# Gated mix of cached attention and a small gated MLP, one decode step: W_down's load ahead of the third K tile, the first K tile loaded from two queues

## The chip, the cores and the metric

The kernel runs on one core of one Trainium2 chip. The core has TensorE (PE), VectorE (DVE), ScalarE (ACT), GpSimd (POOL) and SyncE (SP), and 16 transfer engines (DMA) that move data between HBM and the on-chip memory. Here SyncE and ScalarE issue transfers, each in its own queue. The metric is the device time in microseconds; lower is better. A profile has its own, single execution, whose time need not be the median of the timed runs.

## The reference

One token (x, 448 values) goes through an attention block with a cache of 65,536 positions, 8 key/value heads and 16 query heads of size 256, and through a small gated MLP. A scalar gate mixes both results.

```python
x = A_x
g = sigmoid((x * gate_w).sum(-1, keepdims=True))
# attention: Hq = 16, Hkv = 8, Sk = 65536, Dh = 256
q = (x @ wq).reshape(1, 1, 16, 256)
p = softmax(q . k_cache * 256 ** -0.5)     # each K head serves two query heads
a = (p @ v_cache).reshape(1, 1, 4096) @ wo
# MLP: F = 1792
b = (relu(x @ W_gate) * (x @ W_up)) @ W_down
return g * a + (1 - g) * b
```

K and V are 256 MB each in binary megabytes (8 x 65,536 x 256 values of 2 bytes). The weights are small beside them: wq and wo 3.5 MB each, the three MLP matrices about 1.5 MB each.

## The kernel before

**Tiles and buffers.** K and V of every head are cut into four tiles (NTH = 4), 32 K tiles and 32 V tiles in all (NT = 32). A tile is 128 partitions by 64 KB, 8 MB. Three buffers of that size, `ring[0]` to `ring[2]`, hold what is loaded. K tiles alternate between `ring[1]` and `ring[2]` (`place`, L406): K0 in `ring[1]`, K1 in `ring[2]`, K2 in `ring[1]` again, and so on. V tiles, but for the last four, go to `ring[0]`. Before the first V tile, `ring[0]` holds the weights side by side: wq in its front part (L346, L347), W_gate and W_up in that same part once the query is made (L350, L351), and W_down behind wq (L349), in a part that nothing else uses until the MLP is over.

**The order of the loads.** The list `order` (L381) names the loads in the order in which SyncE issues them, each with its planned duration in us. From it follow the due times `tL`. SyncE's program is in that order, and an issue that has to wait holds up every issue behind it. K tile n (L680) waits until the scores of tile n - 2 are made, since it overwrites that buffer (`free`, L564). W_gate and W_up (L640, L642) wait until the query is made. W_down (L675) waits for nothing. V0 (L772) waits until the MLP is over.

**The order on the engines.** Every operation has an engine and a key; each engine's program is sorted by key (`finish`), and waits on semaphores are put in where an operation depends on another engine or on a transfer. So an engine works strictly in the order of the keys. ScalarE's queue begins with the loads of x (L421, key -9) and of gate_w (L422, key -8), 0.9 KB each.

**What happens to the first K tile.** VectorE begins with constants (keys below 0.1), then makes x's transposed copies with TensorE (L478 to L494, keys 0.5 to 0.91, from x), then the gate: product with gate_w (L464, key 1), sum, exponential on ScalarE (L466), reciprocal and difference (L468 to L470), a broadcast through TensorE (L471, L472) and L475 (key 1.9). Behind these come the four transposes of K0 in place (L682 with `f_trans`, keys from 22.35 on). TensorE meanwhile multiplies x by wq (`f_q`, L497 to L503), ScalarE copies the query (L630), VectorE turns it (L632) and spreads it (`f_xm`), ScalarE copies it to `xcur` (L634), and TensorE makes the scores (`f_qk`, L531 to L544) in two halves. VectorE takes the maximum of each row (L703) and ScalarE the exponential (L705). Then follow the transposes of K1.

Every fourth K tile closes a head: the maxima are brought together, the probabilities scaled and transposed, and the products with V (L584) follow as the V tiles land. At the end come the last V tile in three pieces, wo in six, and the output.

Of the kernel before, what the change touches and what calls it, by code (L numbers as in the profile page):

```python
# [27 lines left out]
class _Plan:  # L28
# [8 lines left out]
    def op(self, eng, key, fn, deps=(), tag=None):  # L37
        eng, cls = {"pv": ("pe", "pv"), "dx": ("dv", "dx"), "ap": ("ac", "ap")}.get(eng, (eng, eng))
        o = _Op(eng, key, fn, deps, tag=tag, cls=cls)
        self.ops.append(o)  # L40
        return o

    def dma(self, eng, key, sem, fn, deps=()):
        if sem not in self.dsem:
            self.dsem[sem] = self.es.enter_context(self.nc.semaphore("d_" + sem))
        o = _Op(eng, key, fn, deps, dma=sem)
        self.ops.append(o)
        return o
# [212 lines left out]
def bass_gated_mix__gqa_block_cached__glu_gated_reglu__decode_kernel(  # L261
# [35 lines left out]
    with es:  # L297
# [3 lines left out]
        ring = [sb("ring%d" % i, [128, U * DH], BF) for i in range(NRING)]  # L301
# [69 lines left out]
        op, dma = pl.op, pl.dma  # L371
# [6 lines left out]


        TILE = 19.35  # L380
        order = [("k", 0, TILE), ("wq", 0, 8.7), ("k", 1, TILE), ("k", 2, TILE), ("wd", 0, 3.8), ("gu", 0, 7.7)]  # L381
        for n in range(3, NT):
            order.append(("k", n, TILE))
            if n >= NTH:
# [10 lines left out]
        t = 3.0  # L395
# [10 lines left out]
        def place(kind, i):  # L406
            if kind == "k":
                return 1 + i % 2
            if kind == "v":
                return 1 + i % 2 if i >= NT - NTH else 0  # L410
            return {"vp": 2, "wo": 0}[kind]

        for kind, i, _ in order:
            if kind in ("k", "v") or (kind, i) in (("wo", 0), ("vp", 0)):
                r = place(kind, i)
# [101 lines left out]
        def k_src(n):  # L517
            h, t_ = divmod(n, NTH)
            return A_k_cache[0, h, :, :].rearrange("(p t u) d -> p t (u d)", t=NTH, u=U)[:, t_, :]
# [7 lines left out]
        def f_trans(sl, w):  # L527
            v = ring[sl][:, w * 8192:(w + 1) * 8192].bitcast(U32)
            return lambda e: e.transpose(v, v)  # L529
# [34 lines left out]
        def free(key):  # L564
            out_ = []
            for f in freed[key]:
                out_.append(l_[f] if isinstance(f, str) else qk[f[1], 1] if f[0] == "k" else pv[f[1]])
            return out_
# [55 lines left out]
        for kind, i, t in sorted(issue, key=lambda q: q[0] != "wq"):  # L624
# [51 lines left out]
            elif kind == "k":  # L676
                n = i
                h, t_ = divmod(n, NTH)
                sl = slot["k", n]
                kd = dma("sp", t, "r%d" % sl, lambda e, n=n, sl=sl: e.dma_start(ring[sl][:], k_src(n)), free(("k", n)))  # L680
                tk = max(tL["k", n], last.get("free", 0))
                tr = [op("dv", tk + 4.5 * w, f_trans(sl, w), [kd]) for w in range(4)]  # L682
                if n > 1:
                    tr[1].deps.append(aexp[n - 2])
                if t_ == 0:
# [82 lines left out]
            elif kind in ("v", "vp"):  # L768
                if kind == "v":
                    n, lo, hi = i, 0, U  # L770
                    sl = slot["v", n]
                    dep = dma("sp", t, "r%d" % sl, lambda e, sl=sl, n=n: e.dma_start(ring[sl][:], v_src(n)), free(("v", n)))  # L772
                else:
                    n, (lo, hi) = NT - 1, PIECES[i]
                    sl = slot["vp", 0]
# [96 lines left out]
```

## Time and profile before

| | |
|---|---|
| time, median of 3 runs | 1278.07 us (1277.55 to 1278.48) |
| time of the profiled execution | 1279.05 us |
| its span | 1277.2 us |
| HBM read in the span | 549.03 MB, 430 GB/s |
| VectorE busy | 630.0 us (49%) |
| TensorE busy | 359.1 us (28%) |
| ScalarE busy | 78.0 us (6%) |

The span goes from the first to the last instruction of the core; the profiled execution's time is 1.85 us longer. The strips of the page show the span in 40 slices of about 32 us, with a digit for each tenth of busy share. In the lists, a row begins with its start and its duration in us, then come the engine and the line of the kernel, and what ended the idle time before it. A "q" behind an engine's name (SPq, ACTq) marks what that engine's sequencer issues, here transfers. The views of stretches give busy time per engine, then the granted clock of TensorE, the share of the 16 transfer engines, and the rate.

### The profile page before, as it was taken

Reading aid. Unit: us, or ns where it says so; the run is one execution under the profiler, and the core shown is the slowest. Engines: PE = TensorE matmul, PEld = TensorE weight load, DVE = VectorE, ACT = ScalarE, POOL = GpSimd, SP = SyncE. Lnnn points to the kernel's source line nnn. Section 1 sums busy time; section 2 is a strip of 40 time slices with the busy share of each in tenths; the row PEclk is TensorE's granted clock in tenths of the full one; section 3 lists DMA queues with packets and bytes.
Section 4 is the critical chain, followed back from the end, with each engine's and each line's share of the span. In section 5 each row is a group of like instructions: output and inputs, shape, how many; then the busy total and the mean of one; then the engine's idle time right before and its main releaser. Section 6 shows DMA issues by size and latency. Waiting matters only on the chain.

```text
span 1277.2 us, 10244 instructions
## 1 busy us (share of the span) xinstructions
PE 359.1 (28%) x4505; PEld 150.8 (12%) x4505; DVE 630.0 (49%) x309; ACT 78.0 (6%) x163; POOL 4.6 (0%) x23
## 2 busy tenths in 40 slices
PE   0533420142220323212322321233302233202525
PEld 0111110021100111101111110111100111001202
DVE  4776655553555633557334575335554355554300
ACT  0000100010000100001000010000000010000100
POOL 1000000000000000000000000000000000000000
PEclk9756655666655666656666556666556666566667
DMA  9999999999999999999999999999999999999998
GB/s 411 395 438 433 429 427 433 443 435 429 427 433 441 437 429 427 433 441 435 431 427 433 441 435 431 427 433 443 433 431 427 435 441 433 431 427 435 441 418 364
DMA packets 11389, 549.13 MB, mean 430 GB/s; under 512 B 1267, under 2 KB 1654, under 8 KB 2294
## 3 DMA queue, kind: packets, MB, share of 16 engines
q1 hardware_dynamic: 11378, 549.03, 99.5%
q8 instruction: 4, 0.07, 0.0%
q14 instruction: 3, 0.02, 0.0%
q10 hardware_dynamic: 4, 0.00, 0.0%
HBM read 549.03 MB, written 0.00 MB: 430 GB/s over the span
## 4 chain that ended last, share of the span: by engine, by line
DMA 80%; PE 15%; DVE 3%; ACT 1%; issue 1%; SPq 0%; another core or an unknown queue 0%; ACTq 0%
DMA ring<-in_A_v_cache_dram 74%; PE O L584 13%; DMA ring<-in_A_wo_dram 3%; DVE ring L529 3%; DMA ring<-in_A_wq_dram 2%; PE ST L540 1%; ACT pcur L591 1%; PE O L501 1%; SPq L785 0%; PE A_ps L551 0%; SPq L776 0%; DVE nmb L703 0%; DVE ring L660 0%; PE A_ps L653 0%
## 5 line engine op out<-in xcount | busy, mean ns | idle before, releaser
L529 DVE STREAM_TRANSPOSE ring<-ring 128x4096 uint32<-128x4096 uint32 x128 | 557.5, 4413 | 207.5 <-DMA ring<-in_A_k_cache_dram 207.5
L584 PE MATMUL O<-ring,pcur 128*4 128x512 bf16 x2048 | 179.5, 527 | 795.8 <-ACT pcur L591 786.9
L703 DVE TENSOR_REDUCE nmb<-ST 128x1 f32<-128x512 f32 x32 | 22.1, 692 | 339.2 <-PE ST L540 339.2
L584 PEld LDWEIGHTS O<-ring,pcur 128*4 128x4 bf16 x2048 | 57.6, 108 | 917.9 <-ACT pcur L591 803.2
L540 PE MATMUL ST<-ring,xcur 128*16 128x512 bf16 x2048 | 136.5, 419 | 47.9 <-DVE ring L529 47.3
L540 PEld LDWEIGHTS ST<-ring,xcur 128*16 128x16 bf16 x2048 | 64.5, 92 | 113.6 <-DVE ring L529 51.8
L705 ACT ACTIVATE P_sb<-ST,nmb 128x512 bf16<-128x512 f32 x32 | 44.5, 1392 | 362.7 <-DVE nmb L703 362.7
L591 ACT COPY pcur<-ptp 128x256 bf16<-128x256 bf16 x32 | 13.2, 415 | 741.1 <-DMA ring<-in_A_v_cache_dram 741.1
L607 DVE TENSOR_SCALAR o_sb<-O,rcm 128x256 bf16<-128x256 f32 x8 | 3.8, 478 | 60.9 <-PE O L584 60.9
L730 DVE TENSOR_TENSOR P_sb<-P_sb,hs 128x1024 bf16<-128x1024 bf16 x16 | 18.9, 1222 | 7.9 <-ACT hs L724 7.9
L735 PE MATMUL PT<-identb,P_sb 128*128 128x128 bf16 x128 | 14.3, 279 | 17.5 <-DVE P_sb L730 17.3
L501 PE MATMUL O<-ring,P_sb 128*128 128x512 bf16 x28 | 8.6, 479 | 17.6 <-DMA ring<-in_A_wq_dram 17.6
L735 PEld LDWEIGHTS PT<-identb,P_sb 128*128 128x128 bf16 x128 | 10.4, 124 | 19.9 <-DVE P_sb L730 19.9
L744 ACT COPY ptp<-PT 128x256 bf16<-128x256 bf16 x32 | 10.3, 375 | 22.7 <-PE PT L735 22.7
L705 ACT ACTIVATION_READ_ACCUMULATOR P_sb<-ST,nmb 128x1 f32 x32 | 8.3, 258 | 0.0
L501 PEld LDWEIGHTS O<-ring,P_sb 128*128 128x128 bf16 x28 | 3.2, 118 | 22.5 <-issue 20.7
L551 PE MATMUL A_ps<-ring,attnA 128*1 128x224 bf16 x64 | 5.2, 319 | 1.2 <-DMA ring<-in_A_wo_dram 1.1
L756 DVE RECIPROCAL rc<-M_ps 128x2 f32<-128x2 f32 x8 | 1.4, 170 | 7.5 <-PE M_ps L755 7.5
L719 PE MATMUL M_ps<-identf,hs 128*2 128x128 f32 x8 | 2.2, 270 | 9.9 <-DVE hs L717 9.9
L571 PE MATMUL O<-zer,identb 128*128 128x512 bf16 x8 | 4.7, 587 | 0.0
L755 PE MATMUL M_ps<-hs,ones_f 128*128 128x2 f32 x16 | 4.5, 352 | 0.0
L557 PE MATMUL A_ps<-o_sb,ecur 128*128 128x32 bf16 x64 | 3.2, 191 | 3.1 <-DVE o_sb L610 3.1
(94 smaller groups left out, 69.9 us busy)
## 6 DMA issues: line engine op xcount, KB each, us to landing
ring<-in_A_v_cache_dram SPq DMA_DIRECT2D x1, 4096.0 KB, 23.6
ring<-in_A_wq_dram SPq DMA_DIRECT2D x1, 3072.0 KB, 29.0
ring<-in_A_v_cache_dram SPq DMA_DIRECT2D x1, 3072.0 KB, 30.6
ring<-in_B_W_down_dram SPq DMA_DIRECT2D x1, 1568.0 KB, 25.8
ring<-in_B_W_gate_dram SPq DMA_DIRECT2D x1, 1344.0 KB, 28.1
ring<-in_B_W_up_dram SPq DMA_DIRECT2D x1, 1344.0 KB, 30.1
ring<-in_A_wo_dram SPq DMA_DIRECT2D x1, 1232.0 KB, 34.7
ring<-in_A_v_cache_dram SPq DMA_DIRECT2D x1, 1024.0 KB, 32.2
```

The costliest lines, as they stand in the source:

```text
L501: ins = e.matmul(QN_ps, xw3[:, kt, 31 - m:159 - m], rhs, start=(kt == 0 and m == 0), stop=(kt == R3 and m == J // 4 - 1))
L529: return lambda e: e.transpose(v, v)
L540: ins = e.matmul(bank[32 * w:32 * w + 16, :], xcur[:, x0:x0 + 16], ktv[sl][:, u0:u0 + 16, c, :, r_], start=(b == 0 and c == 0 and r_ == 0) ...
L551: ins = e.matmul(A_ps[32 * g:32 * g + 1, 0:D2], lhsT, rhs[:, g * D2:(g + 1) * D2], start=start, stop=stop, skip_group_check=True, tile_pos ...
L571: last["zo", h] = op("pv", key, lambda e: e.matmul(OP[:], identb[:, :], zer[:, 0:1].to_broadcast([128, 512]), start=True, stop=True, skip_ ...
L584: ins = e.matmul(OP[32 * g:32 * g + 4, :], pcur[a % 2][:, 4 * k:4 * k + 4], ring[sl][:, k * 512:(k + 1) * 512], start=False, stop=False, s ...
L591: pc[n] = op("ap", max(tp - 5, last["tev", h] - 0.5), lambda e: e.copy(pcur[a % 2][:].rearrange("p (k i) -> p k i", i=4), ptp[:].rearrange ...
L703: smax[n] = op("dv", sx, lambda e, n=n, t_=t_: e.tensor_reduce(NM[:, t_:t_ + 1], ST[n % 2][:], AX.X, ALU.max, negate=True), [qk[n, 1], las ...
L705: aexp[n] = op("ac", sx + 1, lambda e, n=n, t_=t_: e.activation(P_sb[:, t_:2048:4], ST[n % 2][:], ACTF.Exp, bias=NM[:, t_:t_ + 1], scale=1 ...
L730: rsc = op("dv", tt, lambda e, pb=pb: e.tensor_tensor(pb, pb, X[:, 12:16].unsqueeze(1).to_broadcast([128, 256, 4]), ALU.mult), [h7, aexp[n]])
L735: ins = e.transpose(PT[rd][:, s * 128:(s + 1) * 128], P_sb[:, (rd * 8 + s) * 128:(rd * 8 + s + 1) * 128], identb[:, :])
L744: ins = e.copy(dst, src)
```

## The change

Two edits. In `order`, W_down (`wd`) changes places with K2, so that SyncE issues it behind K1 and ahead of K2. And K0 is no longer issued as one transfer of 128 partitions: SyncE issues partitions 0 to 63 in its old place, and ScalarE issues partitions 64 to 127, with key -10 and a semaphore of its own (`k0`). The transposes of K0 depend on both transfers. The other K tiles are issued as before.

```diff
-        order = [("k", 0, TILE), ("wq", 0, 8.7), ("k", 1, TILE), ("k", 2, TILE), ("wd", 0, 3.8), ("gu", 0, 7.7)]
+        order = [("k", 0, TILE), ("wq", 0, 8.7), ("k", 1, TILE), ("wd", 0, 3.8), ("k", 2, TILE), ("gu", 0, 7.7)]
...
-                kd = dma("sp", t, "r%d" % sl, lambda e, n=n, sl=sl: e.dma_start(ring[sl][:], k_src(n)), free(("k", n)))
+                rows_ = slice(0, 64 if n == 0 else 128)
+                kd = dma("sp", t, "r%d" % sl, lambda e, n=n, sl=sl, rows_=rows_: e.dma_start(
+                    ring[sl][rows_, :], k_src(n)[rows_, :]), free(("k", n)))
+                kds = [kd] if n else [kd, dma("ac", -10, "k0", lambda e, sl=sl: e.dma_start(ring[sl][64:128, :], k_src(0)[64:128, :]))]
                 tk = max(tL["k", n], last.get("free", 0))
-                tr = [op("dv", tk + 4.5 * w, f_trans(sl, w), [kd]) for w in range(4)]
+                tr = [op("dv", tk + 4.5 * w, f_trans(sl, w), kds) for w in range(4)]
```

## The prediction

> **What bounds the kernel now.** I read first the head of the page, then the start in order of time, then the transfers where the first hole shows.
>
> ```profile
> span 1277.2 us, 10244 instructions
> PE 359.1 (28%) x4505; PEld 150.8 (12%) x4505; DVE 630.0 (49%) x309; ACT 78.0 (6%) x163; POOL 4.6 (0%) x23
> DMA  9999999999999999999999999999999999999998
> GB/s 411 395 438 433 429 427 433 443 435 429 427 433 441 437 429 427 433 441 435 431 427 433 441 435 431 427 433 443 433 431 427 435 441 433 431 427 435 441 418 364
> DMA packets 11389, 549.13 MB, mean 430 GB/s; under 512 B 1267, under 2 KB 1654, under 8 KB 2294
> ```
>
> No engine is over half busy, while the 16 transfer engines are full in every slice: 549 MB at 430 GB/s is the span. Every byte stays in the changed kernel, so the time can only move by time in which the transfer engines stand still. The second slice (395) is the only one in the body that falls well below the rest, so I looked there.
>
> ```profile
> 0.71 0.53 ACTq L421 DMA_DIRECT2D P_sb<-in_A_x_dram  x1
> 0.72 0.41 SPq L680 DMA_DIRECT2D ring<-in_A_k_cache_dram  x1
> 1.28 0.21 ACTq L422 DMA_DIRECT2D scr<-in_gate_w_dram  x1
> 4.92 0.18 DVE L478 COPY scr<-P_sb 1x64 bf16<-1x64 bf16 x1
> 6.04 0.18 DVE L494 COPY P_sb<-xT 128x4 bf16<-128x4 bf16 x1
> 9.99 0.61 DVE L464 TENSOR_TENSOR ptp<-P_sb,scr 1x448 f32<-1x448 bf16 x1 [3.77 <-DMA scr<-in_gate_w_dram]
> 11.33 1.28 ACT L466 ACT_TABLE_LOAD   x1 [11.33 <-DVE gz L465]
> 14.23 0.23 DVE L475 TENSOR_SCALAR mg<-emat,gb 128x4 f32<-128x4 bf16 x1
> 22.89 17.42 DVE L529 STREAM_TRANSPOSE ring<-ring 128x4096 uint32<-128x4096 uint32 x4 [8.42 <-DMA ring<-in_A_k_cache_dram]
> 31.55 8.56 PE L501 MATMUL O<-ring,P_sb 128*128 128x512 bf16 x28 [17.55 <-DMA ring<-in_A_wq_dram]
> 36.20 3.41 PEld L501 LDWEIGHTS O<-ring,P_sb 128*128 128x128 bf16 x16 [0.28 <-issue]
> 40.20 0.59 ACT L630 CAST ptp<-O 128x512 bf16<-128x512 f32 x1 [27.38 <-PE O L501]
> 40.82 0.45 DVE L632 STREAM_TRANSPOSE scr<-ptp 128x256 uint32<-128x256 uint32 x1 [0.51 <-ACT ptp L630]
> 44.33 6.46 PE L540 MATMUL ST<-ring,xcur 128*16 128x512 bf16 x64 [0.65 <-issue]
> 50.83 0.33 SPq L680 DMA_DIRECT2D ring<-in_A_k_cache_dram  x1
> 51.20 0.43 SPq L675 DMA_DIRECT2D ring<-in_B_W_down_dram  x1
> ```
>
> Columns are start, duration, engine, line, tile. K0 lands at 22.9, VectorE transposes it in place for 17.4 us, turns the query at 40.82, and TensorE makes the scores until 50.8. Only then may SyncE issue K2 (50.83), because it overwrites K0's buffer. W_down stands behind K2 in SyncE's queue and so isn't issued before 51.20, although nothing holds it. Does that leave the transfer engines idle? The next view shows stretches, the last three columns being TensorE's clock, the share of transfer time and the rate. A packet counts in the stretch where it starts.
>
> ```profile
> 44.50:45.00 0.50, 0.50 (x8) 0.14 (x4) 0.00 (x0) 0.00 (x0) 0.00 (x0) 0.50 3.32 1442
> 45.00:45.50 0.50, 0.50 (x8) 0.14 (x4) 0.00 (x0) 0.00 (x0) 0.00 (x0) 0.50 1.21 524
> 45.50:46.00 0.50, 0.50 (x9) 0.14 (x4) 0.00 (x0) 0.00 (x0) 0.00 (x0) 0.50 0.30 131
> 47.00:47.50 0.50, 0.50 (x12) 0.14 (x4) 0.00 (x0) 0.00 (x0) 0.00 (x0) 0.50 3.32 1442
> 47.50:48.00 0.50, 0.50 (x8) 0.14 (x4) 0.00 (x0) 0.00 (x0) 0.00 (x0) 0.50 1.04 426
> 49.00:51.50 2.50, 1.79 (x24) 0.53 (x16) 0.67 (x1) 0.00 (x0) 0.00 (x0) 0.80 0.08 26
> 51.50:52.00 0.50, 0.00 (x0) 0.00 (x0) 0.03 (x1) 0.44 (x1) 0.00 (x0) 1.00 3.20 1081
> 52.00:52.50 0.50, 0.00 (x0) 0.00 (x0) 0.16 (x1) 0.50 (x1) 0.00 (x0) 1.00 2.73 918
> 52.50:53.00 0.50, 0.00 (x0) 0.00 (x0) 0.50 (x1) 0.46 (x2) 0.00 (x0) 1.00 0.37 131
> ```
>
> A K tile has 128 rows of 64 KB, so each transfer engine moves 8, one per round. A round takes (3.32+1.21+0.30) x 0.5 = 2.42 us. K1's last round starts from 47.0 on, so the next could start at 49.4. K2's starts at 51.5: **2.1 us of standstill**. The first round after it takes (3.20+2.73+0.37) x 0.5 = 3.15 us, 0.7 more than 2.42. Filling this hole wholly is worth about 2.8 us, and I found no other in the body.
>
> **The change part by part.** *W_down ahead of K2.* It has 1792 x 448 values of 2 bytes, 1.606 MB, and at 430 GB/s takes 3.73 us. Issued at about 2.6 us, it runs directly behind K1 and fills the hole if K2 is issued as before; 2.1 us of it are then covered. Call D the delay of K2's issue. The hole becomes 2.1 + D - 3.73. As long as that is positive, everything behind K2 starts D later but has 3.73 us less to move: **time change = D - 3.73**. For D under 1.6 there is no hole and the change is -2.8. W_gate and W_up are still issued behind K2, as before. The issue itself (0.43 us on SyncE) passes a queue that then waits till 50 us for K2, so it costs nothing; on the path it would cost 0.43.
>
> *K0 in two halves.* The bytes and the engines are the same, 4 rows from each queue per transfer engine, so K0 should land near 22.9 as before. ScalarE's issue of the half costs about 0.4 to 0.5 us, as the 0.41 on SyncE and 0.53 on ScalarE; ScalarE has nothing else before 11.33. The real cost is the order on ScalarE's queue: the half has key -10, x -9, gate_w -8. So **x and gate_w, which went first, now stand behind 4 MB**. VectorE runs in key order: x's copies (keys 0.5 to 0.91), the gate (1 to 1.9), then the transposes of K0 (22.35 on). Those must wait for both small loads and the gate chain, with TensorE and ScalarE in it. Before, this chain ended at 14.23 + 0.23 = 14.46, with 8.4 us to spare.
>
> When do the small loads land? Three stretches of the transfer queues (0 to 2, 7 to 8, 9.5 to 10 us) hold all four packets of ScalarE's queue; x's two come first:
>
> ```profile
> q10 hardware_dynamic: 2, 0.00, 0.1%
> ...
> q10 hardware_dynamic: 1, 0.00, 0.3%
> ...
> q10 hardware_dynamic: 1, 0.00, 0.1%
> ```
>
> gate_w's data moved after 7 us and its completion after 9.5, about one round of K0 apart, while K0 was running till 22.9. So a transfer engine takes packets of the two queues by turns, a packet of each. In the changed kernel I assume x and gate_w sit on one transfer engine, behind its four rows of the half: x, its completion, gate_w, its completion, with a packet of W_q between any two. W_q's first 384 rows are loaded as three to a partition (L626), 24,576 B per packet, at 430/16 GB/s 0.91 us each. gate_w is there at 22.89 + 4 x 0.91 = 26.5, x at about 24.7, and x's copies (4.92 to 6.22, 1.3 us) are over by 26.0. Then the gate chain runs, 9.99 to 14.46, so 4.5 us, and the transposes start at **31.0 instead of 22.89, 8.1 later**. They end at 48.4. The query is ready at 40.8 as before (40.20 + 0.59; W_q lands no later, and TensorE's part of the gate lies inside the 4.5 us that end at 31.0, before the 31.55 of W_q's products). Before, the transposes ended at 22.89 + 17.42 = 40.31 and the turn waited till 40.82, a slack of 0.5. So **D = 8.1 - 0.5 = 7.6**, and 7.6 - 3.73 = **+3.9 us**.
>
> Bounds of D. The two small loads cannot land later than W_q if each waits two packets per turn: 4 x 0.91 more, D = 11.2. They cannot be useful earlier than the half itself if they really queue behind it: both at 22.9, chain 1.3 + 4.5, transposes at 28.7, D = 5.3. I take the turns, as gate_w's own packets show them. The scores (6.46 us at half clock) could run faster: W_q's last 16 loads took 3.41 us, 0.21 each, so 16 groups of four would take 3.4 and D would fall by 3.1. Nothing indicates a warm clock after the idle time from 40.1 to 48, so I keep 6.46. The one added wait, a second semaphore, comes ahead of the first transpose; behind it stand the other transposes, the query's turn and mask, and TensorE's scores, all counted in D.
>
> Is a second hole made? SyncE's later issues:
>
> ```profile
> 73.45 21.77 SPq L680 DMA_DIRECT2D ring<-in_A_k_cache_dram  x2
> 100.65 0.33 SPq L772 DMA_DIRECT2D ring<-in_A_v_cache_dram  x1
> 104.04 17.42 DVE L529 STREAM_TRANSPOSE ring<-ring 128x4096 uint32<-128x4096 uint32 x4 [5.11 <-DMA ring<-in_A_k_cache_dram]
> ```
>
> K3 is issued at 73.45, K4 at 73.45 + 21.77 - 0.33 = 94.9. From 51.5 on, K2 (8192 KB by its shape), W_down (1568), W_gate and W_up (3136) take 13.2 MB at 430 GB/s, 30.7 us, till 82.2, and K3 19.5 more, till 101.7: leads of 8.7 and 6.8 us. They shrink by at most 7.6 - 3.9 = 3.7, so both stay covered. From K3 on VectorE waits for transfers again (the 5.11), and the delay of the compute side ends there.
>
> **The rivals.** *The small loads aren't held up* (other side). If the transfer engines take ScalarE's small packets ahead of the half's rows, x and gate_w land in the first 15 us, D is under 1.6 and the hole is gone: -2.8, 1275.3 us. For it: gate_w passed rows of K0 before. Against: those were in another queue; here they are in the same. It decides where gate_w lands before 22.89 - 4.5 + 0.5 + 1.6 = 20.5.
>
> *The small loads come with the half, without turns*: D = 5.3, +1.6, 1279.7 us. For it: x's two packets came together at the start. Against: gate_w's did not.
>
> *The scores run at the full clock*: D = 4.5, +0.8, 1278.9 us.
>
> *Longer turns.* With two packets per turn +7.5; if a whole transfer were drained at each turn, x would follow W_q's eight rows (22.9 + 7.3 = 30.2) and gate_w the next transfer (wq's last 64 rows, 0.5 MB, 1.2 us, 31.4); transposes at 35.9, D = 12.5, +8.8, 1286.9 us. Against it: gate_w's data moved amid K0's eight rounds. The Trainium skill, "DMA: Bandwidth & Descriptors", section "Queues, rings and completion order", says that an engine alternates between the queues per packet, and that such a packet commonly groups some 9 to 17 descriptors; by that grouping the time would be about 1286.9, and the trace of K0, with gate_w in its middle, disagrees. The same page's "Rules for kernel authors" advises against loading disjoint partition halves separately, since they share the same engines; by it the split gains nothing, and the forecast's sum holds no gain for it either.
>
> **How the numbers follow.** The profiled run took 1279.05 us, its span 1277.2; the median is 1278.07, 1 us below. +3.9 gives 1282.95 for such a profiled run and **1282.0** as the median. Chances: forecast 0.68 (its own range, D 6.0 to 9.0: 1280.3 to 1283.4), no hold-up 0.09, without turns 0.10, full clock 0.05, longer turns 0.08. What can be told from no change is 0.2%, 2.6 us, so D above 6.3 or below 1.6. Of the forecast 0.06 lies below +2.6. Slower: 0.62 + 0.08 = 0.70; same: 0.06 + 0.10 + 0.05 = 0.21; faster: 0.09. A range from 1278.8 to 1284.5 leaves out the no hold-up case and the longer turns, and takes in the rest.
>
> **What would show it.** Right: no packet of ScalarE's queue with x or gate_w before 22 us, the gate's first multiply (L464) near 26.5 instead of 9.99, K0's transposes near 31.0 with VectorE waiting for gate_w ahead of L464, the query's turn near 48.5, K2's issue near 58.4, W_down's rows directly behind K1's, then a standstill of about 6 us (2.1 + 7.6 - 3.73), and from 130 us on everything 3.9 later. Wrong: L464 before 15 us, or K2 issued before 53, or a second standstill between 80 and 110 us.

## The result and the profile after

The changed kernel takes **1300.53 us** in the median (1300.2 to 1301.85), the kernel before beside it 1278.28: a ratio of 1.0177 (95% interval 1.0165 to 1.0189), +22.25 us. The prediction had the direction, slower, but 1282.0 us, with a range up to 1284.5. The profiled execution took 1300.2 us, against 1279.05 before.

The head of the page of the changed kernel, to be read against that of before:

```profile
span 1298.4 us, 10238 instructions
PE 359.1 (28%) x4497; PEld 148.7 (11%) x4505; DVE 629.9 (49%) x309; ACT 78.0 (6%) x163; POOL 4.6 (0%) x23
DMA  9889999999999999999999999999999999999998
GB/s 226 343 374 450 420 448 424 438 432 422 448 424 444 426 432 440 422 446 426 438 432 424 446 424 446 426 436 434 422 448 424 438 432 424 448 422 446 426 428 364
DMA packets 11405, 549.13 MB, mean 423 GB/s; under 512 B 1283, under 2 KB 1670, under 8 KB 2310
```

The engines do the same work and the same bytes move. What differs is the rate of the first slices, 226 where 411 stood, while the strip above it says 9: the transfer engines are occupied and move half as much. A busy share of 9 is therefore no sign of the full rate; the two rows have to be read together. From slice 4 on the engines are as full and the rate is on average as before.

The start of the changed kernel in order of time (start, duration, engine, line, tile, what ended the wait):

```profile
0.72 0.56 ACTq L683 DMA_DIRECT2D ring<-in_A_k_cache_dram  x1
0.72 0.57 SPq L681 DMA_DIRECT2D ring<-in_A_k_cache_dram  x1
43.35 0.20 DVE L478 COPY scr<-P_sb 1x64 bf16<-1x64 bf16 x1 [38.35 <-DMA P_sb<-in_A_x_dram]
45.23 0.61 DVE L464 TENSOR_TENSOR ptp<-P_sb,scr 1x448 f32<-1x448 bf16 x1 [0.51 <-DMA scr<-in_gate_w_dram]
49.60 17.42 DVE L529 STREAM_TRANSPOSE ring<-ring 128x4096 uint32<-128x4096 uint32 x4
51.41 9.05 PE L501 MATMUL O<-ring,P_sb 128*128 128x512 bf16 x28 [2.18 <-DMA ring<-in_A_wq_dram]
66.94 0.41 DVE L632 STREAM_TRANSPOSE scr<-ptp 128x256 uint32<-128x256 uint32 x1
70.41 5.62 PE L540 MATMUL ST<-ring,xcur 128*16 128x512 bf16 x64 [0.65 <-issue]
76.08 0.33 SPq L681 DMA_DIRECT2D ring<-in_A_k_cache_dram  x1
```

The order of events is the one that the prediction describes: VectorE waits for x, then for gate_w, then runs the gate and only then the transposes. But all of it comes some 18 to 19 us later than the prediction said, since x waits behind ScalarE's half of K0, and that half comes late. The list of transfer issues gives the time from issue to landing of K0; first the kernel before (whole tile), then the changed one (ScalarE's half):

```profile
ring<-in_A_k_cache_dram SPq DMA_DIRECT2D x1, 22.1
```

```profile
ring<-in_A_k_cache_dram ACTq DMA_DIRECT2D x1, 42.1
```

SyncE's half lands at the same time, 42.3 us after its issue. So the same 8 MB, in two halves, need 20 us more. Stretches of 5 us of the changed kernel (the last two columns are the share of the 16 transfer engines and the rate), and the packets per queue in two of them:

```profile
11.00:16.00 5.00, 0.00 (x0) 0.00 (x0) 0.00 (x0) 0.00 (x0) 0.00 (x0) 1.00 0.98 210
16.00:21.00 5.00, 0.00 (x0) 0.00 (x0) 0.00 (x0) 0.00 (x0) 0.00 (x0) 1.00 0.98 210
```

```profile
q10 hardware_dynamic: 16, 1.05, 98.3%
...
q1 hardware_dynamic: 16, 1.05, 98.3%
```

In the first stretch all 16 transfer engines move one row of ScalarE's queue (q10), in the next all 16 one row of SyncE's (q1), and so it goes on through all eight rounds. A round takes 0.98 x 5 = 4.9 us, where a round of a whole K tile took 2.42. So the two queues do alternate packet by packet, but all engines turn together, and at any time all 16 write into the same 64 partitions. Eight rounds of 4.9 instead of 2.42 are 20 us.

The standstill before K2 in the changed kernel:

```profile
73.00:73.50 0.50, 0.50 (x12) 0.22 (x8) 0.00 (x0) 0.00 (x0) 0.00 (x0) 0.50 0.95 401
73.50:74.00 0.50, 0.50 (x12) 0.16 (x7) 0.00 (x0) 0.00 (x0) 0.00 (x0) 0.50 0.20 49
74.00:76.50 2.50, 2.04 (x33) 0.70 (x24) 0.41 (x1) 0.00 (x0) 0.00 (x0) 0.95 0.00 0
76.50:77.00 0.50, 0.00 (x0) 0.00 (x0) 0.50 (x2) 0.18 (x1) 0.00 (x0) 1.00 0.00 0
77.00:77.50 0.50, 0.00 (x0) 0.00 (x0) 0.50 (x1) 0.50 (x1) 0.00 (x0) 1.00 5.24 1737
```

W_down's last packets start at about 73.6, K2's first at 77.0: some 3 us of standstill, where the prediction had 6.

### The profile page after: what moved, and what is told of

Read it like the earlier page. It is cut to its first block, busy times and chain, and to the rows that moved or that the text cites. A ratio compares the mean times of both kernels' runs of the same rounds, so it can differ in the third digit from the quotient of the medians.

```text
span 1298.4 us, 10238 instructions
## 1 busy us (share of the span) xinstructions
PE 359.1 (28%) x4497; PEld 148.7 (11%) x4505; DVE 629.9 (49%) x309; ACT 78.0 (6%) x163; POOL 4.6 (0%) x23
## 4 chain that ended last, share of the span: by engine, by line
DMA 79%; PE 15%; DVE 3%; issue 1%; ACT 1%; SPq 1%; ACTq 0%
DMA ring<-in_A_v_cache_dram 73%; PE O L584 13%; DMA ring<-in_A_wq_dram 4%; DMA ring<-in_A_wo_dram 3%; DVE ring L529 3%; PE ST L540 1%; ACT pcur L591 1%; PE O L501 1%; SPq L788 0%; PE A_ps L551 0%; SPq L779 0%; DVE nmb L706 0%; DVE ring L660 0%; SPq L626 0%; PE A_ps L653 0%
## 5 line engine op out<-in xcount | busy, mean ns | idle before, releaser
L584 PE MATMUL O<-ring,pcur 128*4 128x512 bf16 x2048 | 183.1, 535 | 795.6 <-ACT pcur L591 786.5
L540 PEld LDWEIGHTS ST<-ring,xcur 128*16 128x16 bf16 x2048 | 61.2, 92 | 112.2 <-DVE ring L529 47.8
```

Of the source, the lines that this page charges most:

```text
L540: ins = e.matmul(bank[32 * w:32 * w + 16, :], xcur[:, x0:x0 + 16], ktv[sl][:, u0:u0 + 16, c, :, r_], start=(b == 0 and c == 0 and r_ == 0) ...
L584: ins = e.matmul(OP[32 * g:32 * g + 4, :], pcur[a % 2][:, 4 * k:4 * k + 4], ring[sl][:, k * 512:(k + 1) * 512], start=False, stop=False, s ...
```

## The experiments

Two theories could give packets of 4.9 us. **64 partitions**: 16 transfer engines that all write into one half of the partitions share a limit of about 210 GB/s. **Two queues**: an engine that takes packets of two queues by turns loses the overlap of one packet with the next. The order on ScalarE's queue and W_down's move have to be priced beside them. The kernels of the experiments are called e1 to e9; their ratios are to the kernel before.

**W_down alone (e1).** Against the kernel before:

```diff
-        order = [("k", 0, TILE), ("wq", 0, 8.7), ("k", 1, TILE), ("k", 2, TILE), ("wd", 0, 3.8), ("gu", 0, 7.7)]
+        order = [("k", 0, TILE), ("wq", 0, 8.7), ("k", 1, TILE), ("wd", 0, 3.8), ("k", 2, TILE), ("gu", 0, 7.7)]
```

> Only the move of W_down is left; K0 is loaded whole by SyncE, x and gate_w go first on ScalarE's queue. Both theories (64 partitions: a transfer into 64 partitions moves at half rate, whatever its queue; two queues: a transfer engine that alternates between two queues moves at half rate) expect K0 at 22.9 us, packets of 64 KB in 2.42 us, the standstill between K1 and K2 gone, and a time 2.8 us under the kernel before, about 1275.4. If the move of W_down itself were what costs 22 us, this run would show it.

Measured: 1276.5 us against 1277.85, ratio 0.9989 (0.998 to 0.9998), so 1.4 us faster (0.3 to 2.6). The stretches around the old standstill, in this kernel:

```profile
50.00:51.00 1.00, 1.00 (x16) 0.27 (x8) 0.00 (x0) 0.00 (x0) 0.00 (x0) 0.70 1.07 443
51.00:52.00 1.00, 0.20 (x4) 0.00 (x0) 0.69 (x1) 0.02 (x1) 0.00 (x0) 1.00 1.03 426
52.00:53.00 1.00, 0.00 (x0) 0.00 (x0) 0.72 (x1) 1.00 (x1) 0.00 (x0) 1.00 1.00 426
```

Nothing stands still any more, so the step does what was said; the gain is half of the 2.8 us expected, just outside its interval. It isn't the cause of the loss. This is also the fastest version here, faster than both kernels.

**The two halves from one queue (e2).** Against the changed kernel; `order` is that of before, with W_down behind K2:

```diff
-                kds = [kd] if n else [kd, dma("ac", -10, "k0", lambda e, sl=sl: e.dma_start(ring[sl][64:128, :], k_src(0)[64:128, :]))]
+                kds = [kd] if n else [kd, dma("sp", t + 0.005, "k0", lambda e, sl=sl: e.dma_start(ring[sl][64:128, :], k_src(0)[64:128, :]))]
```

> K0 in the same two halves of 64 partitions, but both issued by SyncE, one behind the other; W_down in its old place behind K2, x and gate_w first on ScalarE's queue. 64 partitions: K0's packets take about 4.9 us, K0 lands near 42 instead of 22.9, everything behind is 19.4 later, about 1297.5. Two queues: packets take 2.42 us, K0 lands at 22.9, the time is that of before, 1278.

Measured: 1299.42 us, ratio 1.0169 (1.0153 to 1.0184). Two stretches of it, one of the first half and the first round of the second half, and K0's transposes:

```profile
11.00:16.00 5.00, 0.00 (x0) 0.00 (x0) 1.35 (x3) 1.49 (x2) 0.00 (x0) 1.00 1.03 210
...
21.00:26.00 5.00, 0.00 (x0) 0.00 (x0) 0.00 (x0) 0.00 (x0) 0.00 (x0) 1.00 0.99 210
```

```profile
44.13 17.42 DVE L529 STREAM_TRANSPOSE ring<-ring 128x4096 uint32<-128x4096 uint32 x4 [26.66 <-DMA ring<-in_A_k_cache_dram]
```

The same 210 GB/s with one queue alone, x and gate_w early. "Two queues" falls. K0 lands 21.2 us later than before, and the time is 21.6 us longer; both were expected at 19.4.

**K0 by columns from two queues (e3).** Against the changed kernel:

```diff
-                rows_ = slice(0, 64 if n == 0 else 128)
-                kd = dma("sp", t, "r%d" % sl, lambda e, n=n, sl=sl, rows_=rows_: e.dma_start(
-                    ring[sl][rows_, :], k_src(n)[rows_, :]), free(("k", n)))
-                kds = [kd] if n else [kd, dma("ac", -10, "k0", lambda e, sl=sl: e.dma_start(ring[sl][64:128, :], k_src(0)[64:128, :]))]
+                cols_ = slice(0, 16384 if n == 0 else 32768)
+                kd = dma("sp", t, "r%d" % sl, lambda e, n=n, sl=sl, cols_=cols_: e.dma_start(
+                    ring[sl][:, cols_], k_src(n)[:, cols_]), free(("k", n)))
+                kds = [kd] if n else [kd, dma("ac", -10, "k0", lambda e, sl=sl: e.dma_start(ring[sl][:, 16384:32768], k_src(0)[:, 16384:32768]))]
```

> The changed kernel, but K0 is cut by columns: SyncE loads the first 32 KB of all 128 partitions, ScalarE (still ahead of x and gate_w) the other 32 KB. 64 partitions: packets of 32 KB take 1.2 us, K0 lands near 22.9, only the order on ScalarE's queue is left, so the gate's first multiply comes near 26, K2 about 6 us later than before, and the time is +2 to +4, 1280 to 1282. Two queues: packets of 32 KB take 2.4 us, K0 lands near 42, the time is that of the changed kernel, 1300.5.

Measured: 1281.28 us, ratio 1.0027 (1.0017 to 1.0037). Its head and its start:

```profile
GB/s 410 380 429 444 439 427 431 427 443 439 427 431 429 443 437 429 429 431 443 435 429 429 437 439 433 429 429 439 439 431 429 429 441 437 431 431 427 443 421 367
```

```profile
24.86 0.61 DVE L464 TENSOR_TENSOR ptp<-P_sb,scr 1x448 f32<-1x448 bf16 x1 [0.49 <-DMA scr<-in_gate_w_dram]
29.24 17.41 DVE L529 STREAM_TRANSPOSE ring<-ring 128x4096 uint32<-128x4096 uint32 x4
50.05 5.38 PE L540 MATMUL ST<-ring,xcur 128*16 128x512 bf16 x64 [0.65 <-issue]
55.49 0.33 SPq L681 DMA_DIRECT2D ring<-in_A_k_cache_dram  x1
```

Two queues, the half ahead of the small loads, W_down moved: everything of the change but the cut by partitions. The first slice is at its 410 again, and the median is 19.25 us below the changed kernel (18.8 if each is taken against its own runs of before). That is the price of the cut by partitions.

**The half behind the small loads (e4).** Against the changed kernel:

```diff
-                kds = [kd] if n else [kd, dma("ac", -10, "k0", lambda e, sl=sl: e.dma_start(ring[sl][64:128, :], k_src(0)[64:128, :]))]
+                kds = [kd] if n else [kd, dma("ac", -7, "k0", lambda e, sl=sl: e.dma_start(ring[sl][64:128, :], k_src(0)[64:128, :]))]
```

> The changed kernel with one key altered: ScalarE issues its half of K0 behind x and gate_w instead of ahead of them. Both theories: K0 still lands near 42 (half rate), but its transposes start there instead of at 49.6, W_down fills the standstill, and the time is 19.4 - 2.8 = +16.6, about 1295. What is missing to the 1300.5 of the changed kernel, about 5.5 us, is the price of the order on ScalarE's queue. If that order were the main cost, the time would fall to near 1278.

Measured: 1296.93 us, ratio 1.015 (1.0134 to 1.0166), 3.6 us under the changed kernel, where 5.5 was expected; the rest of the loss stays. The trace shows where the difference went:

```profile
45.24 17.42 DVE L529 STREAM_TRANSPOSE ring<-ring 128x4096 uint32<-128x4096 uint32 x4 [27.74 <-DMA ring<-in_A_k_cache_dram]
```

ScalarE's half, issued at 1.53 us, lands 43.6 us later, at 45.1; SyncE's is there at 38.2, and the last packets of the other then stand among those of W_q. In the changed kernel K0 was there at 43.0. So the 3.6 us are a net price: the transposes no longer wait 6.6 us (from 43.0 to 49.60) for the gate, but K0 itself comes some 2 us later, so that they start only 4.4 us earlier.

Two questions were left: is it the number of partitions or which ones, and is it the destination or the rows that are read? Three kernels, e5 to e7, one run each, cut K0 anew from the kernel before, all issued by SyncE. `PARTS` lists partitions written and rows read. Of e5 the main lines are shown (its transposes depend on all of `kds`), of e6 and e7 only the line of `PARTS`, in which they differ from e5:

```diff
-                kd = dma("sp", t, "r%d" % sl, lambda e, n=n, sl=sl: e.dma_start(ring[sl][:], k_src(n)), free(("k", n)))
+                PARTS = [(slice(32, 96), slice(32, 96)), (slice(0, 32), slice(0, 32)), (slice(96, 128), slice(96, 128))]
+                kds = [dma("sp", t + 0.001 * q, "k0%d" % q if n == 0 else "r%d" % sl, lambda e, n=n, sl=sl, a=a, b=b: e.dma_start(
+                    ring[sl][a, :], k_src(n)[b, :]), free(("k", n))) for q, (a, b) in enumerate(PARTS if n == 0 else [(slice(0, 128), slice(0, 128))])]
```

```diff
+                PARTS = [(slice(32, 96), slice(0, 64)), (slice(0, 32), slice(64, 96)), (slice(96, 128), slice(96, 128))]
```

```diff
+                PARTS = [(slice(0, 128, 2), slice(0, 128, 2)), (slice(1, 128, 2), slice(1, 128, 2))]
```

> The kernel before, with K0 issued by SyncE in three transfers: partitions 32 to 95, then 0 to 31, then 96 to 127. Theory ports (the port map of the on-chip memory: partitions 32 to 63 reach the eight ports of the lower half, 64 to 95 the eight of the upper half, so 64 partitions around the middle reach all sixteen): the first transfer's packets take 2.4 us, those of the two outer quarters 4.9; K0 lands near 32 and the time is about 1287.5. Theory count (any transfer of 64 partitions is slow, wherever they lie): all packets at 4.9 or worse, K0 at 42 or later, 1297.5 or more.

> As e5_middle_partitions, but the first transfer reads rows 0 to 63 of K0, which the changed kernel's first half reads, into partitions 32 to 95; the second reads rows 64 to 95 into partitions 0 to 31. K0's rows thus stand in other partitions than their values of V, so this run's sum pairs a part of the keys of one head with other values. Theory destination: the first transfer's packets stay at 2.4 us, the time at 1287.5. Theory source (reading rows 0 to 63 of the HBM tensor is what is slow): the first transfer's packets take 4.9 us and K0 lands near 42.

> The kernel before, with K0 issued by SyncE in two transfers, even partitions and odd partitions. If it is only the half of the memory (below and above partition 64) that counts, both reach both halves at all times: 2.4 us a packet, 1278. If each transfer engine takes four successive rows of a transfer, sixteen engines stand on eight ports of the port map at any time (8 partitions apart, every second group of four): 4.9 us a packet, 1297.5.

Measured, one time each: 1290.04, 1288.99 and 1278.39 us, with runs of before at 1277.64 to 1278.66. Stretches of one round each, first of e5 (the second and the sixth round), then of e6 (the third and the sixth), then of e7 (the second, of the even partitions, and the sixth, of the odd ones):

```profile
5.00:7.00 2.00, 0.27 (x5) 0.21 (x5) 0.69 (x6) 0.00 (x0) 1.23 (x6) 1.00 1.21 525
...
16.60:21.50 4.90, 0.00 (x0) 0.00 (x0) 0.00 (x0) 0.00 (x0) 0.00 (x0) 1.00 1.04 214
```

```profile
7.40:9.60 2.20, 0.00 (x0) 0.00 (x0) 1.22 (x2) 0.16 (x1) 0.00 (x0) 1.00 1.10 477
...
16.50:21.60 5.10, 0.00 (x0) 0.00 (x0) 0.00 (x0) 0.00 (x0) 0.00 (x0) 1.00 1.00 206
```

```profile
5.00:7.40 2.40, 0.27 (x5) 0.22 (x5) 0.69 (x6) 0.00 (x0) 1.23 (x6) 1.00 1.02 437
...
14.70:17.10 2.40, 0.00 (x0) 0.00 (x0) 0.00 (x0) 0.00 (x0) 0.00 (x0) 1.00 1.01 437
```

Share times length is the duration of a round: 64 partitions around the middle take 1.21 x 2.00 = 2.42 us, a quarter at the edge 1.04 x 4.90 = 5.1. In e6 the middle takes 1.10 x 2.20 = 2.42 although it reads the rows that the changed kernel's slow half reads; so the rows read don't matter, the partitions written do. Even partitions alone take 1.02 x 2.40 = 2.45, odd ones alone 1.01 x 2.40 = 2.42. A transfer of 64 partitions is at full rate if it covers both sides of partition 64, and at half rate if it lies on one side. A quarter on one side is hardly slower than a half (5.1 against 4.9). The times of e5 and e6, 12 and 11 us above before, lie over the 9.5 that was expected: K0's four rounds at the edges take 4 x (5.1 - 2.42) = 10.7 us more.

The Trainium skill, "SBUF — State Buffer", section "Door 1: The DMA port swizzle (why `[64,N]` ≈ `[32,N]`)", says this: the memory has 16 ports for transfers, partitions 0 to 63 reach only the even eight and 64 to 127 the odd eight, so 64 partitions on one side are no faster than 32. It gives about 218 GB/s for large transfers into eight ports; the traces have 206 to 214. For e7 my expectation also named a slow case, four successive rows of a transfer on each engine, with engines doubled up on ports; the full rate rules that out, and how the 64 even rows are dealt out to the engines stays open.

**Both edits without the two costs (e8).** Against e3, key -7 instead of -10:

> Both edits of the change without its two costs: W_down ahead of K2, K0 by columns from two queues, and ScalarE's part behind x and gate_w. K0 lands near 22.9, the gate is over before that, the standstill is filled: the time of e1_wdown_only, 1276.5. If two queues in themselves cost something, it is above that.

Measured: 1277.13 us, ratio 0.9993 (0.9984 to 1.0003). It is 0.6 us above W_down alone, within the spread of both, so the two queues cost nothing in the time that can be told here. But K0 did not land near 22.9:

```profile
25.92 17.42 DVE L529 STREAM_TRANSPOSE ring<-ring 128x4096 uint32<-128x4096 uint32 x4 [13.81 <-DMA ring<-in_A_k_cache_dram]
53.24 0.33 SPq L681 DMA_DIRECT2D ring<-in_A_k_cache_dram  x1
```

As in e4, ScalarE's part lands late, here 3 us, because its last packets stand among those of W_q; K2 is issued 53.24 - 50.83 = 2.4 us later than before. W_down's 3.73 us more than make up for that. What e8 would cost without W_down's move was not run.

**The order on ScalarE's queue alone (e9).** Against e3, W_down back behind K2:

> The order on ScalarE's queue alone: K0 by columns from two queues with ScalarE's part ahead of x and gate_w, W_down in its old place behind K2. Nothing fills the standstill before K2, so the time is that of before plus the whole delay D of K2's issue. With D of 4.7, as the profile of e3_columns_two_queues has it, 1282.7; with D of 7.1, which the median of e3_columns_two_queues asks for if W_down's move is worth 3.73, 1285.1.

Measured: 1284.66 us, ratio 1.0052 (1.0035 to 1.0068), so +6.8 (4.5 to 8.7). The profiled execution of it took 1284.74, 5.7 over that of before, and its K2 comes later by about as much:

```profile
25.23 0.61 DVE L464 TENSOR_TENSOR ptp<-P_sb,scr 1x448 f32<-1x448 bf16 x1 [0.51 <-DMA scr<-in_gate_w_dram]
29.62 17.41 DVE L529 STREAM_TRANSPOSE ring<-ring 128x4096 uint32<-128x4096 uint32 x4
50.42 6.36 PE L540 MATMUL ST<-ring,xcur 128*16 128x512 bf16 x64 [0.65 <-issue]
56.82 0.33 SPq L681 DMA_DIRECT2D ring<-in_A_k_cache_dram  x1
```

D is 56.82 - 50.83 = 6.0; the medians lie nearer to the second of the two values expected. e3 lies 3.4 below this kernel: with a standstill long enough, W_down's move is worth about its 3.73 us. So the way from before over e9 and e3 to the changed kernel has three steps: 6.8 for the order, 3.4 back for W_down, 19.25 for the cut by partitions. Their sum, 22.65, must come near the 22.25 measured, since each step starts where the last one ends; it splits the loss and is no test. A second price of the cut, from other kernels, is e4 against e8: 19.8.

## Why the prediction was wrong, step by step

**The step that failed** is the first sentence on K0: "The bytes and the engines are the same, 4 rows from each queue per transfer engine, so K0 should land near 22.9 as before." The duration of a row, 2.42 us, came from transfers of 128 partitions, and the trace of before holds no large one of 64. I carried it over without a bound from the other side, and none of the rivals had a slower K0. The runs show 4.9 us for a row where all engines write into one half. K0 landed at 42.8 (0.72 + 42.1) and 43.0 (0.72 + 42.3), 20 us later. With it falls the premise that "the time can only move by time in which the transfer engines stand still": here they were 98% busy and moved half as much. The prediction also cites a row of the Trainium skill, "DMA: Bandwidth & Descriptors", section "Rules for kernel authors", against loading disjoint partition halves separately. I took it as a rule about gains and didn't ask what a half costs when both are never written at once.

**The small loads' order** was right: x and gate_w came behind the half, VectorE waited for them, and the transposes stood behind the gate. Its size was too large. Where K0 lands as before (e9), the gate's first multiply came at 25.23, not 26.5: the turns cost some 2.2 us behind K0 (0.72 + 22.3 = 23.0), not 3.6. The gate took 29.62 - 25.23 = 4.4 against 4.5. D was 6.0 there, not 7.6. In e3 the scores also ran in 5.38 instead of 6.46 us and D was 4.7; the prediction had named faster scores as a bound and kept 6.46. The median of e3, the change with K0 as fast as assumed, is 3.4 us above before, close to the forecast of 3.9. That is partly luck, since D was forecast too long.

**Time change = D - 3.73** holds, though most of D is slow transfer here. In the changed kernel D is 76.08 - 50.83 = 25.25, which gives +21.5; the profiled executions differ by 21.15, the medians by 22.25. Without W_down's move the change is D itself: 6.0 against 5.7 between the profiled executions in e9, and in e2, where K2 is issued at 71.08, 20.25 against 20.26. For e3 the profiled execution is the lowest of its eight runs, 1279.52 (+0.5; the rule gives +0.9); the other seven, of which there is no profile, are 0.7 to 2.7 us above it.

**W_down's move** fills the standstill, as said. At 2.8 us it was over-sized: alone it brings 1.4. What takes the rest wasn't tried and stays open. In the trace of before one transfer engine moves a packet of instructions at 47.5 to 48.5, and a last row of K1 starts only at 49.0 to 49.5. If that is the same engine, it had hardly a standstill of its own, which could be it.

**No second standstill** was right: slices 4 to 39 of the changed kernel are as full as before.

**No hold-up** and **longer turns** are out: VectorE had x at 43.35 in the changed kernel, behind the half, and gate_w 1.9 us, about two packets of W_q of 0.91 us, after it, not after a whole transfer.

## What to carry to other kernels

Before a load is cut, ask which partitions its packets write at the same time: cut a tile by columns, or by even and odd partitions, not at partition 64. Ask also what the cut is to bring: here no cut of K0 was faster than K0 whole, and W_down's move alone (e1) was the fastest. A row's duration is safe to carry over only to a transfer that reaches the same partitions. And a large load that is put first in a queue holds up every small one behind it; here these fed the first instructions of a whole chain, and the price was 3.6 us (e4) to 6.8 us (e9).

## What the runs showed of the hardware

A transfer into partitions 0 to 63 or 64 to 127 moves 210 GB/s; one into 32 to 95, or into the even or the odd partitions, moves a row of 64 KB in some 2.42 us on each engine, the full rate of about 430 GB/s. Two transfers into the two halves, issued at the same time from two queues, don't complement each other: the 16 transfer engines keep in step, all in the one half for 4.9 us and then all in the other, and stay at 210 GB/s. And the strip of the busy share still shows 9 for the slice in which that happens.
